# GpSimd instead of SyncE holds the final wait for the output store in a single-core decode kernel

## The chip, the cores and the metric

The kernel runs on one core of a Trainium2 chip. The metric is the device time of one execution in microseconds. Names of the engines: PE is TensorE, DVE is VectorE, ACT is ScalarE, POOL is GpSimd, SP is SyncE; a name with q behind it is the engine's instruction sequencer.

## The reference, cut to what matters

One token goes through attention with a cache of 65,536 positions, four key/value heads and 32 query heads, and beside it through a mixer with two small and two large projections; the two results and the residual are added.

```python
x = A_x
xn = _layernorm(x, axis=-1)
return x + _A_ref(xn, A_k_cache, A_v_cache, A_wq, A_wo) + _B_ref(xn, B_w1, B_w2, B_w3, B_w4)
```

The output is one row of 1024 bf16 numbers, 2 KB. The inputs are 170 MB, of which the two caches are 134 MB.

## The kernel before

The kernel keeps one list of instructions per engine (`q_pe`, `q_dve`, `q_act`, `q_pool`, `q_sp`). A wait for an event is put into the list of the engine that must wait, and becomes a `wait_ge` on that engine:

```python
def wait_all(self, evs, in_order=False):
    evs = [e for e in set(evs) if self.known.get(e[0], 0) < e[1] and not (in_order and e[0] is self.sem)]
    for e in sorted(evs, key=lambda e: (e[0].name, e[1])):
        ...
        self.ops.append((0, e[0], e[1]))
        self.merge(e)

def emit(self, eng, ops=None):
    for o in self.ops if ops is None else ops:
        if o[0] == 0:
            eng.wait_ge(o[1], o[2])                 # line 73
        ...
```

The end of the program adds the last weights' product to the output row in PSUM, casts it, stores it, and waits until the store has landed:

```python
_op(q_pool, lambda e: e.memset(pT_f[0:64, 0, :], 0.0), writes=[b_pT[0]])          # line 642
resid_rows()
wo_rows()
for i, (r0, nr) in enumerate(w4_parts):
    out_rows([...], [b_W4[i], b_gh], last=(i == len(w4_parts) - 1))
_op(q_dve, lambda e: e.tensor_copy(orow[:, :], OUT), reads=[b_OUT], writes=[b_orow])   # 647
ev_out = _dma(q_sp, chan("out"), lambda e: e.dma_start(out=out[0, 0, :].rearrange("(j n) -> j n", j=4),
              in_=orow[0:97:32, :]), reads=[b_orow])                                    # 648
q_sp.wait_all([ev_out])                                                                 # 649
```

Of the kernel before, what the change touches and what calls it, by code (L numbers as in the profile page):

```python
# [138 lines left out]
def _dma(q, chan, fn, reads=(), writes=(), partial=False):  # L139
    _deps(q, reads, writes)  # L140
    chan.n += 1
    ev = q.dma(fn, chan.sem, 16 * chan.n)
    _done(ev, reads, writes, partial)
    return ev


def bass_parallel_sum__gqa_block_cached__mixer_s_mlp__decode_kernel(
# [31 lines left out]
    with ExitStack() as es:  # L179
# [8 lines left out]
        def sem(name):  # L188
            return E(nc.semaphore(name))
# [80 lines left out]
        q_pool = _Q("pool", sem("c_pool"))  # L270
        q_sp = _Q("sp", None)
        chans = {}

        def chan(name):
            if name not in chans:
                chans[name] = _DmaChan(sem("d_" + name))
            return chans[name]
# [368 lines left out]
            out_rows([(gh_bf[:, r:r + 1], KV[:, 2, r * D:(r + 1) * D]) for r in range(r0, r0 + nr)], [b_W4[i], b_gh], last=(i == len(w4_parts) - 1))  # L646
        _op(q_dve, lambda e: e.tensor_copy(orow[:, :], OUT), reads=[b_OUT], writes=[b_orow])
        ev_out = _dma(q_sp, chan("out"), lambda e: e.dma_start(out=out[0, 0, :].rearrange("(j n) -> j n", j=4), in_=orow[0:97:32, :]), reads=[b_orow])
        q_sp.wait_all([ev_out])

        code = nc.m.functions[0].blocks[0].instructions
        heads = {e: next(i for i in code if i.opcode == "Drain" and i.engine == e) for e in (nc.sync.engine, nc.scalar.engine)}
# [90 lines left out]
```

## Time and profile before

| what | value | where from |
|---|---|---|
| time | 400.30 us, median of 3 (400.28 to 400.30) | the runs |
| first to last instruction ("span") | 399.08 us | the trace |
| time beyond the span | 1.25 us (400.33 - 399.08) | the profiled execution |
| HBM read | 169.87 MB at 426 GB/s | the page |
| SyncE's wait for the store | 1.0 us, ends at 399.08 us | the waits |

This kernel is bound by its stream of data up to the last microseconds: the DMA engines are busy at 80% or more in every slice of the page but the last (50 to 59%), with a mean of 426 GB/s. The change lies behind the stream, so the page's shares say nothing about it. What matters is the order of the last events. Because the time is 1.25 us longer than the span, what comes outside the span may matter too. The prediction shows these lines.

The profile's views list instructions. The trace also has a record of every update of a semaphore, and these go on for 1.4 us after the last instruction (399.081 to 400.516 us). No view prints them; lists in plain fences below are read from those records. The records as kept name a semaphore and a time, not an engine or a value: which engine makes an increment is read from the times of the instructions, and "resets" is the name for the run of writes to semaphores 7 to 255 between the two rounds.

### The profile page before, as it was taken

What the parts mean: (1) busy time and instruction counts of PE and PEld (TensorE: products, weight loads), DVE (VectorE), ACT (ScalarE), POOL (GpSimd) and SP (SyncE); (2) the same over time, 40 slices, a digit from 0 to 9 for tenths busy, and PEclk for the clock granted to TensorE, in tenths of its full rate; (3) what the DMA queues carried; (4) which work ended last, traced back from release to release, by engine and by line L of the source; (5) the groups of instructions that cost most, each with busy time, mean ns of one, the idle gap of its engine ahead of it and who ended that gap; (6) DMA issues with size and microseconds to landing.
All of it is one profiled execution on the core that took longest, in us unless ns stands there. A gap on an engine that the chain in (4) does not pass through costs nothing.

```text
span 399.1 us, 3429 instructions
## 1 busy us (share of the span) xinstructions
PE 168.9 (42%) x1523; PEld 59.0 (15%) x1484; DVE 221.4 (55%) x260; ACT 23.9 (6%) x50; POOL 7.7 (2%) x31
## 2 busy tenths in 40 slices
PE   0034767338033713460357036413541362137394
PEld 0011334012001210110012001101120110012232
DVE  0024222994298549833984597269647952895201
ACT  1000000011001100110011002000100110011000
POOL 5000000000000000000000000000000000000000
PEclk9998568555655665575557555855585558555969
DMA  9999899999999999999999999999999999999995
GB/s 420 420 388 493 383 441 466 447 415 427 420 427 429 434 460 434 434 427 420 434 427 420 466 440 434 421 420 434 427 427 466 434 440 420 420 427 434 418 414 229
DMA packets 3759, 169.97 MB, mean 426 GB/s; under 512 B 548, under 2 KB 552, under 8 KB 808
## 3 DMA queue, kind: packets, MB, share of 16 engines
q1 hardware_dynamic: 3608, 169.87, 98.7%
q8 instruction: 5, 0.08, 0.1%
q10 hardware_dynamic: 144, 0.00, 0.0%
q14 instruction: 2, 0.02, 0.0%
HBM read 169.87 MB, written 0.00 MB: 426 GB/s over the span
## 4 chain that ended last, share of the span: by engine, by line
DMA 59%; DVE 25%; PE 12%; issue 1%; ACT 1%; SPq 1%; POOL 0%
DMA KV<-in_A_k_cache_dram 45%; DVE KV L460 18%; DMA KV<-in_B_w_dram 8%; DMA KV<-in_A_x_dram 6%; PE S_ps L411 3%; PE OT_ps L518 2%; DVE mrow L481 2%; PE M_ps L426 2%; PE S_ps L474 2%; PE S_ps L379 1%; ACT p_sb L496 1%; DVE Yall L395 1%; DVE pT_f L509 1%; DVE pT_f L419 1%; PE PT_ps L505 0%
## 5 line engine op out<-in xcount | busy, mean ns | idle before, releaser
L460 DVE STREAM_TRANSPOSE KV<-KV 128x4096 f32<-128x4096 f32 x32 | 140.3, 4422 | 44.3 <-DMA KV<-in_A_k_cache_dram 44.3
L474 PE MATMUL S_ps<-KV,Ycur 128*32 128x512 bf16 x512 | 60.7, 624 | 132.5 <-DVE KV L460 132.5
L518 PE MATMUL OT_ps<-KV,pT_f 128*32 128x512 bf16 x512 | 47.2, 511 | 4.0 <-issue 3.0
L474 PEld LDWEIGHTS S_ps<-KV,Ycur 128*32 128x32 bf16 x512 | 14.3, 126 | 160.0 <-DVE KV L460 142.4
L496 ACT ACTIVATE p_sb<-S_ps,brun 128x1024 bf16<-128x1024 f32 x16 | 17.8, 1114 | 276.6 <-DVE brun L494 176.1
L509 DVE STREAM_TRANSPOSE pT_f<-PT_ps 128x512 f32<-128x512 f32 x32 | 22.5, 702 | 14.0 <-PE PT_ps L505 14.0
L481 DVE TENSOR_REDUCE mrow<-S_ps 128x1 f32<-128x1024 f32 x16 | 19.3, 1205 | 11.3 <-PE S_ps L474 11.3
L484 PE MATMUL M_ps<-Rm,Lmat 128*128 128x16 bf16 x16 | 3.1, 194 | 38.0 <-DVE Rm L482 38.0
L529 DVE SCALAR_TENSOR_TENSOR O_acc<-O_acc,ff,OT_ps 128x512 f32<-128x512 f32 x12 | 9.0, 748 | 14.7 <-PE OT_ps L518 14.7
L518 PEld LDWEIGHTS OT_ps<-KV,pT_f 128*32 128x32 bf16 x512 | 13.1, 115 | 23.8 <-issue 16.4
L411 PE MATMUL S_ps<-KV 128*32 128x512 bf16 x88 | 12.1, 538 | 2.7 <-DVE KV L359 2.7
L339 DVE CAST KV<-KV 128x8 f32<-128x8 bf16 x1 | 0.2, 172 | 22.2 <-DMA KV<-in_A_x_dram 22.2
L578 PE MATMUL S_ps<-KV,o_bf 128*1 128x512 bf16 x64 | 9.9, 484 | 4.5 <-DMA KV<-in_A_wo_dram 4.5
L505 PE MATMUL PT_ps<-p_sb,permR 128*128 128x512 bf16 x16 | 9.7, 607 | 0.8
L426 PE MATMUL M_ps<-ident_f,pT_f 64*128 64x2 f32 (+2 forms) x32 | 7.9, 373 | 2.5 <-DVE pT_f L419 2.5
L484 PEld LDWEIGHTS M_ps<-Rm,Lmat 128*128 128x128 bf16 x16 | 1.7, 104 | 49.3 <-DVE Rm L482 49.3
L582 DVE COPY pT_f<-S_ps 1x512 f32<-1x512 f32 x1 | 0.7, 679 | 14.4 <-PE S_ps L578 14.4
L426 PEld LDWEIGHTS M_ps<-ident_f,pT_f 64*128 64x128 f32 (+2 forms) x32 | 7.7, 326 | 4.7 <-DVE pT_f L419 3.1
L419 DVE COPY pT_f<-S_ps 64x512 f32<-64x512 f32 (+1 forms) x3 | 2.1, 685 | 10.8 <-PE S_ps L411 10.8
L505 PEld LDWEIGHTS PT_ps<-p_sb,permR 128*128 128x128 bf16 x32 | 3.3, 102 | 27.5 <-ACT p_sb L496 14.7
L364 PE MATMUL M_ps<-KV 8*128 8x8 bf16 x1 | 0.2, 184 | 16.1 <-DVE Dmat_f L363 16.1
L642 POOL MEMSET pT_f<- 64x512 f32 x1 | 0.5, 520 | 312.4 <-PE OT_ps L518 312.4
(88 smaller groups left out, 90.2 us busy)
## 6 DMA issues: line engine op xcount, KB each, us to landing
KV<-in_B_w_dram SPq DMA_DIRECT2D x1, 7168.0 KB, 48.0
KV<-in_B_w_dram SPq DMA_DIRECT2D x1, 4352.0 KB, 27.4
KV<-in_B_w_dram SPq DMA_DIRECT2D x2, 2048.0 KB, 28.3
KV<-in_B_w_dram SPq DMA_DIRECT2D x1, 1792.0 KB, 31.3
KV<-in_B_w_dram SPq DMA_DIRECT2D x1, 768.0 KB, 32.7
KV<-in_B_w_dram SPq DMA_DIRECT2D x1, 256.0 KB, 32.9
KV<-in_A_k_cache_dram SPq DMA_DIRECT2D x8, 46.7
KV<-in_A_v_cache_dram SPq DMA_DIRECT2D x8, 28.1
```

The costliest lines, as they stand in the source:

```text
L411: fns.append(lambda e, j=j, k=k, mv=mv: e.matmul(S_ps[32 * (k % 4):32 * (k % 4) + 32, bank + k // 4, :], vec[:, j:j + 1].broadcast_to([P, ...
L419: _op(q_dve, lambda e, b=b, nb=nb: e.tensor_copy(pT_f[0:32 * nb, b, :], S_ps[0:32 * nb, bank + b, :]), reads=[b_S[bank + b]], writes=[b_pT ...
L426: fns.append(lambda e, b=b, nb=nb, c=c: e.matmul(M_ps[:, c0 + 16 * b + c:c0 + 16 * b + 4 * nb:4], pT_f[0:32 * nb, b, c:512:4], ident_f[0:3 ...
L460: _op(q_dve, lambda e: e.transpose(out=KV32[:, s, o:o + 4096], in_=KV32[:, s, o:o + 4096]), reads=[b_KV[s][sub]], writes=[b_KV[s][sub]], l ...
L474: fns.append(lambda e, we=we, cm=cm, mv=mv: e.matmul(S_ps[32 * cm:32 * cm + 32, n % 4, :], Ycur[:, we, :, :].rearrange("p a g -> p (a g)") ...
L481: _op(q_dve, lambda e: e.reduce_max(mrow[:, k:k + 1], S_ps[:, 2 * k:2 * k + 2, :].rearrange("p b c -> p (b c)"), axis=AX.X), reads=b_S[2 * ...
L496: _op(q_act, lambda e: e.activation(p_sb[:, :, :].rearrange("p b c -> p (b c)"), S_ps[:, 2 * k:2 * k + 2, :].rearrange("p b c -> p (b c)") ...
L505: _op(q_pe, lambda e: e.matmul(PT_ps[:, :], permR[:, :], p_sb[:, n % 2, :], start=True, stop=True), reads=[b_p[n % 2], b_const], writes=[b ...
L509: _op(q_dve, lambda e: e.transpose(out=pT_f[:, n % 2, :], in_=PT_ps[:, :]), reads=[b_PT], writes=[b_pT[n % 2]], loop=True)
L518: fns.append(lambda e, q=q, q4=q4: e.matmul(OT_ps[32 * q4:32 * q4 + 32, g % 2, :], pT_bf[:, n % 2, q, :, 1], KV[:, s, 8192 * sub + 512 * q ...
L529: _op(q_dve, lambda e: e.scalar_tensor_tensor(out=O_acc[:, 0:512], in0=O_acc[:, 0:512], scalar=ff[:, k:k + 1], in1=OT_ps[:, k, :], op0=ALU ...
L578: _grp(q_pe, [lambda e, j=j, jj=jj: e.matmul(S_ps[32 * jj:32 * jj + 1, 1, :], o_bf[:, j:j + 1], KV[:, 0, j * D + 512 * jj:j * D + 512 * (j ...
```

## The change

The wait for the output store is put on GpSimd, which has been idle since about 370 us, in place of SyncE, which issues the store. The intent is to let SyncE go as soon as it has issued.

```diff
-        q_sp.wait_all([ev_out])
+        q_pool.wait_all([ev_out])
```

## The prediction

> **What bounds the kernel now.** I read the page first, to see what fills the 400 us, and then only the last three microseconds, since the change touches nothing earlier. The page:
>
> ```profile
> span 399.1 us, 3429 instructions
> PE 168.9 (42%) x1523; PEld 59.0 (15%) x1484; DVE 221.4 (55%) x260; ACT 23.9 (6%) x50; POOL 7.7 (2%) x31
> ...
> DMA  9999899999999999999999999999999999999995
> ...
> HBM read 169.87 MB, written 0.00 MB: 426 GB/s over the span
> ```
>
> The DMA engines are busy in every slice but the last: the kernel is a stream of 170 MB, and no engine is over 55% busy. What happens to the output store can only matter after the stream ends. The timeline of the last microseconds (start, length, engine) shows the end:
>
> ```profile
> 396.60 0.28 PE L566 MATMUL S_ps<-KV,gh_bf 128*1 128x256 bf16 x4 [0.15 <-DMA KV<-in_B_w_dram]
> 396.94 0.42 DVE L647 CAST orow<-S_ps 128x256 bf16<-128x256 f32 x1 [6.78 <-PE S_ps L566]
> 397.39 0.63 SPq L648 DMA_DIRECT2D out_dram<-orow  x1
> ```
>
> It is a strictly serial tail: last weight lands, four matmuls, one cast of 0.42 us, one store issued by SyncE in 0.63 us. The waits of SyncE's queue (us in total, times, longest) and the instructions of the helper line that emits waits tell the rest:
>
> ```profile
> SPq L648 <- DVE orow L647: 33.3, 1, 33.3
> ...
> SPq L73 <- DMA out_dram<-orow: 1.0, 1, 1.0
> ```
>
> ```profile
> L73 SPq EVENT_SEMAPHORE  x1: 17/17/17, 399.1 to 399.1; - x1
> ```
>
> SyncE issues the store, stands 1.0 us at the wait for its landing (398.02 to 399.06), and its 17 ns semaphore instruction, ending at 399.08, is the last instruction of the span. GpSimd's last work is this one (groups of instructions on GpSimd; its own time line puts it at 369.7 us):
>
> ```profile
> L642 POOL MEMSET pT_f<- 64x512 f32 x1 | 0.5, 520 | 312.4 <-PE OT_ps L518 312.4
> ```
>
> So GpSimd has finished some 29 us before the end and can stand at any wait in good time.
>
> The kernel's time (400.28 to 400.30 us) is 1.2 us more than the span (399.08). Something after the last instruction is therefore counted, and the change decides which engine gets there last. The views do not print it, but the trace also holds every update of a semaphore, and those go on after the span. Semaphore 2, which the kernel does not use, is incremented nine times around the end and nine times once more (us from the span's start):
>
> ```
> 1st round: 397.074 397.108 397.147 397.510 | 399.202 399.247 399.285 399.319 399.366
> writes to semaphores 7 to 255:               399.328 ... 399.934
> 2nd round: 400.158 400.192 400.231 400.275 400.298 400.397 400.435 400.469 400.516
> ```
>
> PE's last own update is at 396.912 and the first increment at 397.074; DVE's cast updates at 397.372 and the fourth increment is at 397.510; SyncE's wait starts its 17 ns at 399.064 and the fifth is at 399.202. I read this as a chain through the five engines and back: PE, then ACT and GpSimd (both idle, in an order that I can only guess), DVE, SyncE, and back through DVE, GpSimd, ACT, to PE. An engine that is already standing in the chain passes it on in 34 to 47 ns; DVE and SyncE take 138 ns from the end of their own last business.
>
> [...] the second round takes 400.516 - 400.158 = 0.358 us in eight hops, and between the rounds the semaphores are written in blocks, of which three have 51 numbers. [...] the store's semaphore has one update at 398.399 and four from 398.984 to 399.047, for its four rows of 512 B; whoever waits, the same 399.047 ends the wait. [...] I expect GpSimd's wait to cost what SyncE's does (17 ns here; GpSimd's two semaphore instructions at the program's start also took 17 ns each).
>
> **The change part by part.**
>
> Removed: one wait on SyncE. It ran out at 399.08; SyncE now is done when the issue is, 398.02, and reaches the chain near 398.16 (plus the 138 ns above), where it must wait for GpSimd.
>
> Added: the same wait on GpSimd, for the same semaphore and value, standing ready since 370 us. It ends at 399.064, like SyncE's, because the landing at 399.047 ends both. The span in the profile is unchanged: 399.1 us.
>
> Moved: the last comer of the closing chain. I work out when PE, the last link, is let go, since its block of resets is the last to start and to end (399.585 to 399.934) and it opens the second round.
> - Before: SyncE comes last and stands at the turning point. 399.064 + 0.138 = 399.202, then the way back, 0.045 (DVE) + 0.038 + 0.034 + 0.047 = 0.164: PE is free at 399.366.
> - After: GpSimd's increment, with SyncE's 0.138, is at 399.202 too. But it is on the way out. From the second round: GpSimd to DVE 0.044, DVE to SyncE 0.023; then back to DVE 0.099, not 0.045, because DVE has only just made its own increment and is not yet standing at its second wait (0.112 in the round before the kernel); then 0.038 + 0.034 + 0.047. Sum 0.285 to 0.298, so PE is free at 399.487 to 399.500.
> - Difference: +0.12 to +0.13 us. If GpSimd is the second link and not the third, another 0.039: +0.16 to +0.17.
> After that, 399.366 to 400.516 (1.15 us) shifts as a whole. Nothing else is on the path: no instruction, no transfer, no buffer is released by this wait.
>
> 400.30 + 0.13 = 400.43 us, which is 0.03% slower.
>
> **The rivals.**
> - It gains. SyncE is freed 1.06 us earlier, and if SyncE's own closing work were the longest, that would now lie beside the wait. At most 1.06 us, so 399.2 us. For it: SyncE is the last engine to arrive now. Against it: the block of resets that starts first after SyncE's increment (399.328) is done at 399.416, half a microsecond before the last block[...].
> - It loses more. GpSimd may be slower between a wait and the chain than SyncE's 0.138 us: no row shows GpSimd there coming from a wait. Its drain at the program's start took 179 ns against SyncE's 111, though behind memsets. I allow up to 0.3 us: 400.7 us.
> - Nothing at all: the store's landing sets the end and the clock stops at a point that does not see the order of the chain; 400.3 us. For it: the span will not move. Against it: the 1.2 us that are counted beyond the span are just what the resets and the second round take.
> - A change of the body, by a moved instruction in the streams of SyncE or GpSimd: nothing speaks for it, since both edits are behind everything else on their engines.
>
> **Range and chances.** The working gives 400.42 to 400.47; no gain and no loss gives 400.3; a slow GpSimd 400.7. Three runs of before lie within 0.02 us and its profiled run at 400.33, so the noise within one chip is small against these, but [...] I widen to 400.1 to 400.8. Two per cent are 8 us, seven times the wait that is moved: 0.99 for within 2%, and what is left for a run disturbed by something else, 0.005 either way.
>
> **What would show it.** In the changed profile: the wait for the store among GpSimd's waits, about 29 us long, and none on SyncE; one 17 ns semaphore instruction more on GpSimd, at 399.1; the span within 0.1 us of 399.1. In the semaphore updates: increments one and two (perhaps only one) near 397.1, no more until GpSimd's at 399.20, and then six or seven in a row instead of four after the last comer, ending near 399.49, and the second round ending near 400.64. If the fifth increment followed the third by much less than 67 ns plus, if the return to DVE took 45 ns and not 100, or if GpSimd's came much later than 138 ns after its wait, that step is wrong. A time under 400.2 or over 400.7 in fast runs on the same chip would mean that the closing chain is not what I take it for.

The sum came to 400.30 + 0.13 = 400.43 us, where the 0.12 to 0.13 us are the way of 0.285 to 0.298 us less 0.164 us, and every hop in it is a difference of two records of semaphore 2. The changed kernel shows this much: SyncE's last instruction ends at 398.057 us, and no record of a reset comes before 399.858 us, 0.118 us after the fifth increment. On the range, the medians of before in the four sets of rounds are 400.30, 400.48, 400.41 and 400.48 us.

## The result, and the profile after

| | before | after |
|---|---|---|
| time, us | 400.30, median of 6 (400.28 to 400.65) | 401.03, median of 6 (400.93 to 401.12) |
| ratio | | 1.0017, 95% interval 1.0004 to 1.0029 |
| span of the profiled execution, us | 399.08 | 399.13 |
| its time, us | 400.33 | 400.93 |
| its time beyond the span, us | 1.25 | 1.80 |

A ratio is the mean time of one kernel's runs over the mean of the other's in the same rounds, so it is not quite the ratio of the medians. The kernel became slower by 0.17%, which is "the same" by a limit of 2%, but clear of no change at all, and it lies above the upper end of the predicted range, 400.8 us.

The timeline of the end of the changed kernel (start, length, engine, line):

```profile
396.98 0.43 DVE L647 CAST orow<-S_ps 128x256 bf16<-128x256 f32 x1 [8.40 <-PE S_ps L566]
397.43 0.62 SPq L648 DMA_DIRECT2D out_dram<-orow  x1
```

The instructions of line 73, which emits waits (count, duration in ns least/median/most, first and last start):

```profile
L73 DVEq EVENT_SEMAPHORE  x9: 21/21/21, 100.1 to 374.8; - x9
L73 PEldq EVENT_SEMAPHORE  x6: 51/51/51, 25.5 to 379.4; - x6
L73 POOLq EVENT_SEMAPHORE  x1: 17/17/17, 399.1 to 399.1; - x1
```

The waits of SyncE's queue in the changed kernel end with this line; the one for the store is gone:

```profile
SPq L648 <- DVE orow L647: 33.4, 1, 33.4
...
SPq L728 <- PEq L728: 0.3, 1, 0.3
```

The edit did what it says and nothing else: the store is issued at the same place, the 17 ns instruction has changed its engine, and it still is the last of the span, at 399.1 us. GpSimd's list of waits does not show the new one, although the prediction thought it would: that view counts GpSimd's waits before its own work, and none follows. Of the 0.6 us only 0.05 us lies within the span, and that is the cast, which started at 396.98 us in place of 396.94 us in this execution. The rest is in the closing records, set side by side here (us; the increments of semaphore 2, in order):

```
                 before                                   after
wait ends        399.081 (SyncE)                          399.130 (GpSimd)
first round      397.074 397.108 397.147 397.510          397.119 397.153
                 399.202 399.247 399.285 399.319          399.672 399.717 399.740 399.837
                 399.366                                  399.876 399.912 399.958
resets           399.328 to 399.934                       399.858 to 400.525
second round     400.158 ... 400.516                      400.749 ... 401.107
```

Before, four increments precede the end of the wait and five follow it. After, two precede it and seven follow. The first of the seven comes 0.542 us after GpSimd's wait has ended, where SyncE's came 0.121 us after its own. The last increment comes 0.591 us later than before, and the profiled execution took 0.60 us longer (400.93 - 400.33).

### The profile page after: what moved, and what is told of

The parts are those of the page before. It is cut to its first block, busy times and chain, and to the rows that moved or that the text cites. A ratio compares the mean times of both kernels' runs of the same rounds, so it can differ in the third digit from the quotient of the medians.

```text
span 399.1 us, 3445 instructions
## 1 busy us (share of the span) xinstructions
PE 177.1 (44%) x1539; PEld 59.4 (15%) x1484; DVE 221.3 (55%) x260; ACT 23.9 (6%) x50; POOL 7.7 (2%) x31
## 4 chain that ended last, share of the span: by engine, by line
DMA 58%; DVE 25%; PE 13%; issue 1%; ACT 1%; SPq 0%; POOL 0%
DMA KV<-in_A_k_cache_dram 45%; DVE KV L460 18%; DMA KV<-in_B_w_dram 8%; DMA KV<-in_A_x_dram 6%; PE S_ps L411 3%; PE OT_ps L518 2%; DVE mrow L481 2%; PE M_ps L426 2%; PE S_ps L474 2%; PE S_ps L379 1%; ACT p_sb L496 1%; DVE Yall L395 1%; DVE pT_f L509 1%; PE PT_ps L505 1%; DVE pT_f L419 1%
## 5 line engine op out<-in xcount | busy, mean ns | idle before, releaser
L505 PE MATMUL PT_ps<-p_sb,permR 128*128 128x512 bf16 x32 | 18.9, 590 | 0.8
L578 PE MATMUL S_ps<-KV,o_bf 128*1 128x512 bf16 x64 | 8.4, 428 | 4.5 <-DMA KV<-in_A_wo_dram 4.5
```

What stands on the lines that cost most here:

```text
L505: _op(q_pe, lambda e: e.matmul(PT_ps[:, :], permR[:, :], p_sb[:, n % 2, :], start=True, stop=True), reads=[b_p[n % 2], b_const], writes=[b ...
L578: _grp(q_pe, [lambda e, j=j, jj=jj: e.matmul(S_ps[32 * jj:32 * jj + 1, 1, :], o_bf[:, j:j + 1], KV[:, 0, j * D + 512 * jj:j * D + 512 * (j ...
```

## The experiments

Every kernel below gave the right result. "Arrival" is the time from the end of an engine's last recorded instruction to its increment in the first round. "Way" is from there to the ninth increment. "Rest" is from the ninth increment to the last of the second round. All three are from the trace of one execution, in us. "Beyond" is the mean over all runs of time less span, where the listed spans have one decimal only, so that 0.05 us is about what it can tell. The ratios tell less: 0.6 us is 0.15% of the time, and their intervals reach 0.13% to 0.17% to either side. So the comparisons below rest on "beyond" and on the traces.

| kernel | who comes last | arrival | way | rest | median time (before, same rounds) | beyond (before) |
|---|---|---|---|---|---|---|
| before | SyncE | 0.121 | 0.164 | 1.150 | 400.30 | |
| changed | GpSimd | 0.542 | 0.286 | 1.149 | 401.03 (400.30) | 1.85 |
| both | GpSimd | 0.543 | 0.284 | 1.151 | 401.05 (400.48) | 1.82 (1.28) |
| act | ScalarE | 0.119 | 0.324 | 1.239 | 400.84 (400.48) | 1.71 (1.28) |
| dve | VectorE | 0.146 | 0.241 | 1.150 | 400.40 (400.48) | 1.39 (1.28) |
| pe | TensorE | 0.292 | 0.358 | 1.140 | 400.84 (400.48) | 1.56 (1.28) |
| early | SyncE | 0.121 (GpSimd, not last: 0.543) | 0.162 | 1.145 | 400.44 (400.41) | 1.28 (1.27) |
| hot | GpSimd | 0.542 | 0.286 | 1.146 | 401.08 (400.41) | 1.84 (1.27) |
| drain | GpSimd | 0.529 | 0.286 | 1.238 | 401.16 (400.41) | 1.84 (1.27) |
| fill | GpSimd | 0.542 | 0.286 | 1.148 | 400.94 (400.41) | 1.80 (1.27) |
| again | GpSimd | 0.543 | 0.285 | 1.149 | 401.06 (400.48) | 1.81 (1.28) |
| last | GpSimd | 0.512 | 0.285 | 1.150 | 401.58 (400.48) | 1.80 (1.28) |
| fill2 | GpSimd | 0.532 | 0.285 | 1.146 | 400.99 (400.48) | 1.82 (1.28) |
| act2 | ScalarE | 0.118 | 0.324 | 1.150 | 400.89 (400.48) | 1.64 (1.28) |

My theory after the result was A: GpSimd itself takes 0.42 us longer than SyncE from its last instruction into the closing chain, and the chain from its link costs another 0.12 us. The rivals: B, every engine but SyncE arrives late; C, what costs is that SyncE no longer waits and stands idle.

### both: SyncE waits too

```diff
+        q_sp.wait_all([ev_out])
         q_pool.wait_all([ev_out])
```

> GpSimd and SyncE both wait for the store. Theory A (what costs is GpSimd's arrival: 0.56 us from its wait to its increment of the closing chain, plus two more links): as the changed kernel, about 401.0 us, GpSimd's increment some 0.56 us after its wait, SyncE's right behind DVE's. SyncE's own 0.138 us is over by then. Theory C (what costs is that SyncE no longer waits and stands idle in the chain): as before, 400.3 us.

Measured: 401.05 us, ratio 1.0013 (0.9999 to 1.0026). Both engines stand at the wait:

```profile
L73 SPq EVENT_SEMAPHORE  x1: 17/17/17, 399.2 to 399.2; - x1
L73 POOLq EVENT_SEMAPHORE  x1: 17/17/17, 399.2 to 399.2; - x1
```

With SyncE's wait put back, the closing records still look like the changed kernel's, with GpSimd arriving 0.543 us after its wait. C falls: taking the wait from SyncE costs and gains nothing that can be seen (1.82 us beyond the span here, 1.80 to 1.85 us in the runs of the changed kernel), and giving it to GpSimd costs everything.

### act, dve, pe: the wait on each of the other engines

```diff
-        q_pool.wait_all([ev_out])
+        q_act.wait_all([ev_out])
```

(and likewise `q_dve` and `q_pe`)

> ScalarE alone waits. Theory A (only GpSimd is slow; ScalarE takes about 0.14 us to the chain and is link two): last comer's way to PE 0.039+0.044+0.023+0.10+0.038+0.034+0.047 = 0.325 us against SyncE's 0.164, so +0.16 us, 400.46 us. Theory B (every engine but SyncE takes some 0.56 us from wait to chain): +0.58 us, 400.9 us.

> VectorE alone waits. Theory A: 0.14 us to the chain (as behind its cast before), then 0.023+0.10+0.038+0.034+0.047 = 0.242 us to PE, so +0.08 us, 400.38 us; its wait instruction takes 21 ns. Theory B: +0.5 us, 400.8 us.

> TensorE alone waits: the first link, so that the whole chain runs after the store. Theory A: about 0.16 to 0.2 us to the chain, then the full 0.358 us: +0.22 to +0.26 us, 400.5 to 400.6 us, and all nine increments after 399.2 us. Theory B: +0.6 us, 400.9 us.

The line of waits in each of the three, in that order of kernels; for VectorE and TensorE the count is one more than in the changed kernel, and the last start is the new wait's:

```profile
L73 ACTq EVENT_SEMAPHORE  x1: 17/17/17, 398.9 to 398.9; - x1
```

```profile
L73 DVEq EVENT_SEMAPHORE  x10: 21/21/21, 101.1 to 399.0; - x10
```

```profile
L73 PEldq EVENT_SEMAPHORE  x7: 51/51/51, 25.4 to 399.1; - x7
```

The number of increments before the store's landing names the links one by one: none when TensorE waits, one when ScalarE does, two with GpSimd, three with VectorE, four with SyncE. So the order PE, ACT, POOL, DVE, SP, which the prediction had only inferred and in part guessed, is shown. The ways are 0.358, 0.324, 0.286, 0.241 and 0.164 us, from the first link to the fifth, and the sums of the single hops expected 0.358, 0.325, 0.285 to 0.298, and 0.242. SyncE, at the turning point, has the shortest way, 0.164 us. The order of the way back is not shown by such a count; that it is the reverse is the author's reading, with which the ways agree.

B falls too: ScalarE arrives in 0.119 us and VectorE in 0.146 us. TensorE takes 0.292 us, more than expected. GpSimd's 0.542 us stands alone.

In time, VectorE's variant cannot be told from before (ratio 1.0002, 0.9988 to 1.0015), though its time beyond the span is 0.11 us more. TensorE's was put at 400.5 to 400.6 us and took 400.84 us, with 0.28 us more beyond the span. ScalarE's variant is where A's arithmetic fails: 0.16 us was expected and the time beyond the span grew by 0.43 us. Its arrival and way are as expected, but its rest is 0.09 us longer, and its measured time is another 0.24 us longer than the place of its last increment would give if it lay as in before (see act2).

### early: GpSimd waits, but for the cast

```diff
-        q_pool.wait_all([ev_out])
+        q_pool.wait_all([ev_cast])
+        q_sp.wait_all([ev_out])
```

(`ev_cast` is the event of the cast in line 647.)

> GpSimd waits for the cast of the output row (its semaphore is updated near 397.37 us) as its last step, SyncE waits for the store as before. If GpSimd's 0.56 us from wait to chain is its own and constant, its increment comes near 397.94 us, is hidden behind the store's landing, and the time is that of before (400.3 to 400.5 us). If the 0.56 us belong to the store's semaphore or to the end of the DMA, GpSimd's increment comes some 0.14 us after its wait.

Measured: 400.44 us against 400.41 us, ratio 1.0000 (0.9983 to 1.0017), 1.28 us beyond the span against 1.27 us.

```profile
L73 POOLq EVENT_SEMAPHORE  x1: 17/17/17, 397.5 to 397.5; - x1
L73 SPq EVENT_SEMAPHORE  x1: 17/17/17, 399.2 to 399.2; - x1
```

GpSimd's wait ended at 397.524 us and its increment came at 398.067 us: 0.543 us again. So the time is GpSimd's own, does not depend on whether it waited for the store or for the cast, and when it lies beside the store's landing it costs nothing that can be seen beyond the span. This is the clearest single test: the same 0.54 us, off the path, and the whole loss is gone.

### hot: GpSimd works shortly before its wait

```diff
+        q_pool.wait_all([ev_cast])
+        q_pool.op(lambda e: e.memset(dd[:, 0:1], 0.0))
         q_pool.wait_all([ev_out])
```

> As the changed kernel, but GpSimd runs one tiny memset at about 397.4 us, behind a wait for the cast, and then waits for the store. Theory D (a long idle GpSimd, 29 us, is slow to resume): from wait to chain 0.14 us in place of 0.56, 400.4 to 400.5 us. Theory E (a fixed cost of GpSimd's closing): 0.56 us again, 400.9 to 401.1 us.

The timeline shows that the memset ran 1.6 us before the wait ended, and that it ended 27.55 us of idleness:

```profile
397.59 0.10 POOL L650 MEMSET dd<- 128x1 f32 x1 [27.55 <-DVE orow L647]
```

Measured: arrival 0.542 us, 401.08 us. Long idleness is not the cause; 1.6 us of waiting, as here, gives the same figure as 29 us.

### drain: an explicit drain behind the wait

```diff
         q_pool.wait_all([ev_out])
+        q_pool.op(lambda e: e.drain(), tick=False)
```

> As the changed kernel, with an explicit drain on GpSimd between its wait and the end. It shows when the first instruction after the wait starts and what a drain costs. If the sequencer is slow to resume, the drain starts some 0.4 us after the wait and its end is followed by the chain within 0.15 us: 0.6 us in all. If the closing itself is slow, the drain starts within 0.1 us of the wait, takes 0.05 to 0.2 us, and some 0.5 us or more follow: 401.0 to 401.2 us. If a drain is what is slow, it lasts some 0.4 us and the time is 401.4 us.

```profile
L650 POOLq DRAIN  x1: 41/41/41, 399.2 to 399.2; - x1
```

The build put the wait onto the drain itself, so there is one instruction of 41 ns where there were to be two, and the question when an instruction after the wait starts is not answered. What it does show: the drain began 0.024 us after the store's last update (399.209 us) and ended at 399.274 us. So neither the end of the wait nor this drain is slow, and 0.529 us followed all the same. A drain that the closing itself might hold was not tested.

### fill and fill2: the closing elsewhere in GpSimd's stream

```diff
+        for _ in range(300):
+            q_pool.op(lambda e: e.nop(nofuse=True), tick=False)
```

> As the changed kernel, with 300 empty instructions on GpSimd in its idle time (behind the memset at 370 us), so that the closing instructions lie elsewhere in GpSimd's stream. If the 0.56 us are a fetch of instructions that depends on where the closing lies, the figure changes by tenths of a microsecond. If they are the closing's own, 0.56 us again and 400.9 to 401.1 us.

This experiment failed: the trace has no record of the 300 empty instructions and the same 41 GpSimd records as the changed kernel's, so nothing was moved. Its run is one more of the changed kernel (400.94 us, arrival 0.542 us). The second attempt used waits that are already met:

```diff
+        q_pool.ops += [(0, q_dve.sem, 1)] * 480
```

> The changed kernel with 240 waits that are already met (two semaphores' worth each, so that they survive the compiler) on GpSimd in its idle time, so that its closing lies elsewhere in its instruction stream. A fetch that depends on the place: GpSimd's figure differs from 0.56 us by tenths. The closing's own: 0.56 us, 400.9 to 401.1 us.

```profile
L73 POOLq EVENT_SEMAPHORE  x241: 17/43/43, 370.6 to 399.2; - x121
```

The build joined the waits in pairs, 240 instructions more. The expectation meant that number and words it badly. One of these met waits was joined to the wait for the store, which took 43 ns in place of 17. The stream did get longer: the page of fill2 lists two more packets on an instruction queue than that of the changed kernel (first line), and the DMA records put these two, of 8 KB each, at 377.0 and 388.5 us, while GpSimd ran the added waits:

```profile
q14 instruction: 2, 0.02, 0.0%
q14 instruction: 4, 0.03, 0.0%
```

Arrival was 0.532 us and the time 400.99 us. So this other place in the stream did not change the figure; only one was tried. In the DMA records of all fourteen traces the last packet of an instruction queue starts no later than 394.44 us, so none shows a fetch in the closing. But these records end with the store's packets (at 398.7 us in before), and whether they would show a later one is not known.

### last: real work as GpSimd's last instruction

```diff
         q_pool.wait_all([ev_out])
+        q_pool.op(lambda e: e.memset(pT_f[0:64, 0, :], 0.0), tick=False)
```

> The changed kernel with a memset of some 0.52 us on GpSimd behind its wait, as its last instruction. If GpSimd's closing first lets its engine finish and then takes its 0.54 us, the increment comes about 1.1 us after the wait and the time is 401.5 to 401.6 us. If the 0.54 us are work of the sequencer that runs while the memset does, the increment comes about 0.6 us after the wait and the time stays near 401.0 us.

```profile
L650 POOL MEMSET pT_f<- 64x512 f32 x1 | 0.5, 517 | 28.0 <-DMA out_dram<-orow 28.0
```

The build put the wait onto the memset, as it did with the drain. The memset ended at 399.869 us and the increment came at 400.381 us: 0.512 us after its end and 1.03 us after its start. The time was 401.58 us. GpSimd's closing first lets the engine finish and then takes its half microsecond; it does not lie beside GpSimd's own work.

### again and act2: repeats

> The changed kernel once more, with five rounds. If the trace accounts for all of the loss, the time beyond the span is again 0.55 to 0.6 us more than in the kernel before, the median is 0.55 to 0.75 us over it, and GpSimd's increment comes 0.56 us after its wait starts.

The changed kernel took 401.06 us against 400.48 us, ratio 1.0014 (1.0001 to 1.0028), 0.53 us more beyond the span, arrival 0.543 us. That is just under the 0.55 to 0.6 us expected beyond the span, and within the range expected of the median (0.58 us).

> ScalarE alone waits, once more. In the first run of this kernel ScalarE took only 0.136 us from wait to chain, but the resets of PE began 0.09 us later than elsewhere and the time ended 0.24 us further behind the second round than in the other kernels. If that is systematic, the time beyond the span is again some 0.4 us over that of the kernel before; if it was chance, 0.16 us.

400.89 us, 0.36 us more beyond the span, arrival 0.118 us, way 0.324 us. The longer rest is not there this time (1.150), so it does not belong to the wait on ScalarE; *drain* had it once too. The other part is systematic: in before, changed, both, dve, pe, hot, drain, fill, last, fill2 and again the measured time is the place of the last increment less 0.18 to 0.19 us. In the two runs with the wait on ScalarE it is the last increment plus 0.05 us. (In *early* it is less 0.08 us.) So with the wait on ScalarE something is counted that leaves no record. What it is, and where in the execution it lies, stays open.

## Why the prediction was right or wrong

**What bounds the kernel, and that the span would not move:** right. The span was 399.13 us, 0.05 us more, because the cast started 0.045 us later in that execution, not because of the wait.

**That the closing chain decides, not the wait:** right, and shown. SyncE's freedom brings nothing (both, 1.82 us beyond the span), and which engine comes last sets the time (1.28 us beyond the span with SyncE, 1.80 to 1.85 us with GpSimd). The one part of it that the chain does not explain is the 0.24 us of the two ScalarE runs (and 0.10 us in the profiled execution of early).

**The way from GpSimd's link:** right in place and size. It was put at 0.285 to 0.298 us and measured 0.286 us, against 0.164 us for SyncE. This term of +0.12 us was all that the prediction's sum contained. GpSimd is the third link: two increments precede its own, at 397.119 and 397.153 us. The slow hop behind the fifth increment came as expected, 0.097 us (399.740 to 399.837), where it was 0.045 us before (399.202 to 399.247). The reason given for it, that DVE is not yet standing at its second wait, is the author's reading; the records show that the fourth increment was 0.023 us old at the fifth, and 1.69 us old before.

**"After: GpSimd's increment, with SyncE's 0.138, is at 399.202 too":** this is the step that failed. The mechanism held and the size of one term was off. GpSimd's figure from the start of its wait is 0.559 us (399.113 to 399.672), not 0.138 us. No row of the profile before showed it, since there GpSimd's last instruction ended at 370.2 us, 27 us before the first increment. I took the figure of one engine for another because their wait instructions both take 17 ns. The equal 17 ns is right (399.113 to 399.130 on GpSimd, 399.064 to 399.081 on SyncE) and says nothing about what follows it: 0.542 us and 0.121 us. The 0.138 us itself mixes two starting points: for SyncE it runs from the start of its wait (0.121 us from the end), for VectorE from the cast's update of its semaphore (0.150 us from the cast's end at 397.360). The rival "it loses more" named the weak place, but allowed 0.3 us where 0.42 us was needed, and its 400.7 us, widened to 400.8, set the upper end of the range. The prediction had listed this very sign ("if GpSimd's came much later than 138 ns after its wait, that step is wrong"). Its last sign, that a time over 400.7 us would speak against the closing chain, was too strict: the time was over it with the chain as described.

**The sum, with the measured terms** (profiled executions, in us): later wait +0.049 (399.113 - 399.064), arrival +0.421 (0.559 - 0.138), way +0.122 (0.286 - 0.164), rest -0.001: +0.591. The measured difference of these two executions is +0.60. The medians of the first rounds differ by 0.73 and those of the repeat by 0.58; the runs of before alone vary from 400.23 to 400.73 us in the repeat's rounds, and their spans with them, so what exceeds 0.6 lies within this scatter and is not shown to be the change's. Nor is the later wait, which follows the later cast. What the change itself costs is then 0.421 + 0.122 - 0.001 = 0.54 us, and the repeat's 0.53 us beyond the span agrees.

**The rival of a gain:** wrong as expected. **Nothing at all:** wrong; the measured time does depend on which engine comes last in the chain. **A change in the body:** no sign of one.

**The chances:** 0.99 for within 2% was right. The range of 400.1 to 400.8 us was not, for the reason above.

**What stays open:** what GpSimd does in the half microsecond. It was the same, 0.51 to 0.54 us, with another semaphore waited for (early), after 1.6 us in place of 29 us of idleness (hot), with a drain as the last instruction (drain) and at one other place in the stream (fill2), and it begins only behind GpSimd's last work (last). Its instructions leave no record in the trace, so its cause is not shown. No run varied what GpSimd does earlier in the program, so whether every program pays it, or only one that uses GpSimd in this way, is not shown either. No tried variant beats the kernel before: SyncE has nearly the shortest arrival and the shortest way, and only VectorE's variant cannot be told from it in time.

## What to carry to other kernels

What follows was measured in this one kernel. Here the engine that holds the last wait is followed by the closing chain, and it should be the one with the least behind it. From the end of its wait until the ninth increment it took SyncE 0.285 us, VectorE 0.387, ScalarE 0.443, TensorE 0.650 and GpSimd 0.828. In the time that counts, ScalarE changes places with TensorE, because of its unexplained 0.24 us: beyond the span are 1.28 us with SyncE, 1.39 with VectorE, 1.56 with TensorE, 1.64 to 1.71 with ScalarE and 1.80 to 1.85 with GpSimd. End GpSimd's stream early, ahead of the last event by more than the 0.51 to 0.54 us that it took here (in *early* its wait ended at 397.524 us, about 1.7 us ahead of SyncE's, with 1.28 us beyond the span against 1.27 us), and leave the final wait where it is cheapest. When a change sits behind the last instruction, compare time less span, and do not lend one engine's unrecorded cost to another.
